# Threshold attention and hash routing: the identity ahead of tau, and routing's operations at other places

## The chip, the cores and the metric

The kernel runs on one core of one Trainium2 chip. Its metric is the device time of one execution, in microseconds (us). Lower is better. The kernel before takes 1007.04 us, the median of three runs that lie between 1006.65 and 1007.51. The profile comes from one more execution with a span of 1001.3 us.

The engines are named as in the profile: PE is TensorE (PEld its weight loads), DVE VectorE, ACT ScalarE, POOL GpSimd, SP SyncE, which issues most transfers. L219 is line 219 of the kernel before; in the changed kernel the same statement can stand some lines higher.

## The reference, cut to what matters

Attention in which all scores further than tau below the row's maximum are dropped, and then a layer of eight experts, in which each token goes to the one expert that a hash of its id names:

```python
scores = scale * np.matmul(q, k.transpose(0, 1, 3, 2))          # (8, 8, 576, 576), head_dim 64
thresh = np.max(scores, axis=-1, keepdims=True) - tau
scores = np.where(scores >= thresh, scores, -1000000000.0)
scores = scores - np.max(scores, axis=-1, keepdims=True)
attn = np.exp(scores)
attn = attn / (np.sum(attn, axis=-1, keepdims=True) + 1e-09)
x = np.matmul(attn, v)                                          # then to (4608, 512)
...
expert_idx = token_ids * np.int64(2654435761) % np.int64(E)     # E = 8
for e in range(E):
    mask = expert_idx == e
    h = np.maximum(x[mask] @ w1[e], 0.0)                        # 512 -> 1024
    out[mask] = h @ w2[e]                                       # 1024 -> 512
```

tau is 0.02 in the inputs. A negative tau drops everything; the kernel provides for that with a scale of 0 on k and a large value in `drop`.

## The kernel before: the parts concerned

The kernel treats heads in 32 pairs, each in five steps s = 0 to 4 (n counts all steps, p = n // 5). VectorE negates the scores and takes their extreme (`negate`), ScalarE takes the exponential (`expo`), VectorE masks (`mask`), TensorE turns the weights and multiplies them by v. The routing of the tokens to the experts is computed on the side, in pieces of a generator that hands back control at each `yield`; a second generator writes the token table when the slots are `placed`.

k is scaled by 1/8, or by 0 where tau is negative. Pair 0's k is scaled on VectorE and ScalarE at the start, all later ones on GpSimd:

```python
def scale_k(p):
    nc.gpsimd.tensor_scalar(out=kts[p][:], in0=kts[p][:], scalar1=keep_any[:],
                            scalar2=SCALE, op0=ALU.mult, op1=ALU.mult)
...
# in negate(n, j), after the tile of the last head: the threshold, on GpSimd too
    nc.gpsimd.tensor_scalar(out=thr[:, 0:j + 1], in0=stats[n][0][:, 0:j + 1],
                            scalar1=drop[:], scalar2=None, op0=ALU.add)
```

The start. `make_identity` is two operations on GpSimd. The transposes of the identity keep TensorE busy until there is something to do:

```python
load_pair(1)
make_identity(nc, ident[:])
...                                   # memsets on VectorE
with tc.manual_schedule():
    tr = ps_tr.tile([P, 2, 512], FP32, name="tr")
    for _ in range(16):
        nc.tensor.transpose(tr[:, 0, 0:P], ident[:], ident[:])
    nc.gpsimd.dma_start(out=tau_in[:], in_=...)
    nc.vector.tensor_scalar(out=keep_any[:], in0=tau_in[:], scalar1=0.0, scalar2=None,
                            op0=ALU.is_ge)
    nc.vector.tensor_scalar(out=drop[:], in0=keep_any[:], scalar1=-3e38, scalar2=3e38,
                            op0=ALU.mult, op1=ALU.add)
    nc.vector.tensor_tensor(out=drop[:], in0=drop[:], in1=tau_in[:], op=ALU.max)
    nc.vector.tensor_scalar(out=k_scale[:], in0=keep_any[:], scalar1=SCALE, scalar2=None,
                            op0=ALU.mult)
    nc.vector.tensor_scalar(out=kts[0][:, 0], in0=kts[0][:, 0], scalar1=k_scale[:], ...)
    nc.scalar.activation(kts[0][:, 1], kts[0][:, 1], AF.Copy, scale=k_scale[:])
    constants()
    next(pieces)
    score(0, 0)
```

The order on GpSimd in the built program is: first operation of the identity, tau's transfer, second operation of the identity.

Routing's last pieces make the table of overflow tiles `ov_i`, which is read at the very end of the kernel (and by SyncE's queue as soon as it is there):

```python
    placed.append(True)
    yield
    yield
    nc.vector.tensor_tensor(out=oc, in0=iota_f..., in1=oend..., op=ALU.is_ge)
    yield
    yield
    nc.vector.reduce_sum(ovf[:, 0:NOV], oc, axis=AX.X)
    yield
    nc.vector.tensor_scalar(out=ovf[:, 0:NOV], ..., op0=ALU.min)
    yield
    nc.vector.tensor_copy(ovf[:, NOV:NOV + 1], oend[:, E - 1:E])
    nc.vector.tensor_copy(ov_i[:], ovf[:])
```

In the loop a piece is taken twice in each pair, at s = 3 as the step begins and at s = 0 behind `negate` and `expo`, ahead of `put_xm` (L336). The passage to the experts follows the loop. There the first expert's first product (`early_h`, L579) is computed from the three quarters of x that are there, through the two PSUM buffers of `ps_sc`:

```python
for g in range(4):
    nc.vector.tensor_copy(gidx_x[rows, 1:, 0:n], stok[rows, 1:, KT * g:KT * g + n])
for kt in range(KT):
    fetch_0(kt, HP - 1)
fill(FO * 2 * (CO - 1) - 18)          # TensorE: early_h; VectorE takes each tile out (L586)
```

The memsets of `xh` and `o_last` (L765, L769) stand outside the fixed order and are placed among VectorE's work there.

Of the kernel before, what the change touches and what calls it, by code (L numbers as in the profile page):

```python
# [9 lines left out]
FP32 = mybir.dt.float32  # L10
# [4 lines left out]
ALU = mybir.AluOpType  # L15
# [5 lines left out]
def kernel(  # L21
# [12 lines left out]
    nc = tc.nc  # L34
# [51 lines left out]
    slot_i = consts.tile([P, NTC], I32, name="slot_i")  # L86
    tid32 = consts.tile([P, NTC, 2], I32, name="tid32")
    tau_in = consts.tile([P, 1], FP32, name="tau_in")
    keep_any = consts.tile([P, 1], FP32, name="keep_any")
    k_scale = consts.tile([P, 1], FP32, name="k_scale")  # L90
    drop = consts.tile([P, 1], FP32, name="drop")

# [35 lines left out]
    with tc.tile_pool(name="a_q", bufs=1) as a_q, \  # L128
# [67 lines left out]
                nc.sync.dma_start(out=v_sb[half, 4, half], in_=rows[TAIL:S, half])  # L196

        def scale_k(p):
            nc.gpsimd.tensor_scalar(out=kts[p][:], in0=kts[p][:], scalar1=keep_any[:],
                                    scalar2=SCALE, op0=ALU.mult, op1=ALU.mult)  # L200

        def heads(n):
            return 1 if n % NS == 0 else 2
# [314 lines left out]
                                      offset=0, ap=[[2 * NTC, P], [2, NTC], [1, 2]]))  # L518
        load_v(0)
        load_pair(1)  # L520
        make_identity(nc, ident[:])
        none_f = a_st.tile([P, 1], FP32, name="none_f")
        nc.vector.memset(none_f[:], 0.0)
        for w in w_bufs:
# [9 lines left out]
        def constants():  # L534

            nc.gpsimd.iota(iota_i[:], pattern=[[1, NOV]], base=0, channel_multiplier=0)
            nc.gpsimd.tensor_copy(iota_f[:], iota_i[:])
            make_upper_triangular(nc, u128[:], val=1.0, diag=False)
            nc.gpsimd.memset(ones128[:], 1.0)
            nc.gpsimd.memset(none[:], BIG)  # L540
            nc.gpsimd.memset(gidx[:], BIG)
            nc.gpsimd.memset(gidx_x[:], BIG)
            for t in sidx:
                nc.gpsimd.memset(t[:], BIG)
            nc.gpsimd.iota(tok[:], pattern=[[1, NTC]], base=0, channel_multiplier=NTC)
            for table in slot_dram:
                nc.sync.dma_start(out=table.rearrange("(p c) o -> p (c o)", p=P), in_=none[:])
# [69 lines left out]
                next(h_pieces, None)  # L617

        with tc.manual_schedule():

            tr = ps_tr.tile([P, 2, 512], FP32, name="tr")
            for _ in range(16):
                nc.tensor.transpose(tr[:, 0, 0:P], ident[:], ident[:])
            nc.gpsimd.dma_start(out=tau_in[:],
                                in_=bass.AP(tensor=tau.tensor, offset=0, ap=[[0, P], [1, 1]]))

            nc.vector.tensor_scalar(out=keep_any[:], in0=tau_in[:], scalar1=0.0, scalar2=None,
                                    op0=ALU.is_ge)  # L630
            nc.vector.tensor_scalar(out=drop[:], in0=keep_any[:], scalar1=-3e38, scalar2=3e38,
                                    op0=ALU.mult, op1=ALU.add)
            nc.vector.tensor_tensor(out=drop[:], in0=drop[:], in1=tau_in[:], op=ALU.max)
            nc.vector.tensor_scalar(out=k_scale[:], in0=keep_any[:], scalar1=SCALE, scalar2=None,
                                    op0=ALU.mult)
            nc.vector.tensor_scalar(out=kts[0][:, 0], in0=kts[0][:, 0], scalar1=k_scale[:],
                                    scalar2=None, op0=ALU.mult)
            nc.scalar.activation(kts[0][:, 1], kts[0][:, 1], AF.Copy, scale=k_scale[:])
            constants()
            next(pieces)  # L640
            score(0, 0)
            for n in range(LAST + NS + 1):
                p, s = divmod(n, NS)
                m = n - 2
                if s == 0 and p + 2 < NP:
                    load_pair(p + 2)
                if s == 0 and p + 1 < NP:
                    load_v(p + 1)
                if s == 2 and p in (20, 24):
                    load_w1(p // 4 - 5)  # L650
                if s == 2 and p in (22, 26):
                    load_w2((p - 22) // 4)

                if s == 3 and n < LAST:
                    next(pieces, None)
                if s == 1 and 3 <= p < 2 + KT:
                    nc.sync.dma_start(out=xg_bufs[p - 2][:], in_=xg_bufs[0][:])

                if s == 1 and 2 + KT <= p < 2 + KT + N // DIN:
                    r0 = DIN * (p - 2 - KT)  # L660
                    nc.sync.dma_start(
                        out=x_dram[r0:r0 + DIN, DIN - P:].rearrange("(t p) m -> p t m", p=P),
                        in_=xg_bufs[0][:].rearrange("p (t m) -> p t m", m=P))
                q = p - 1
                if s == 1 and 0 <= q < NP:
                    add_eps(q)
                if s == 1 and p + 1 < NP:
                    scale_k(p + 1)
                if s == 2 and 0 <= q < NP:
                    nc.vector.reciprocal(recs[q][:], recs[q][:])  # L670
                if n == LAST + NS:
                    fill(2)
                if s == 0 and p >= 2:
                    turn_o()
                if n == LAST:
                    for k in (0, 2):
                        tr = ps_sc.tile([P, 2, 512], FP32, name="sc")
                        early_xT(tr, k, k + 2, 0, CO - 1)
                if s in (1, 2) and 0 <= q < NP and n != LAST + 1:
                    av_part(q, 0, ((0, 1, 2), (3, 4))[s - 1])  # L680
                if n < LAST and s in (1, 2):
                    negate(n, 0)
                    expo(n, 0)
                if s == 2 and 0 <= q < NP:
                    put_oT(0)
                if n > LAST:
                    fill(1)
                turned = 0 <= m < LAST
                if turned:
                    tr = turn_w(m, 0)  # L690
                    put_wT(m, 0, tr)
                if n == LAST:
                    put_xm(p - 2)
                    av_part(q, 0, (0, 1, 2))
                if n >= LAST:
                    fill(1)
                if n == LAST:
                    tr = ps_sc.tile([P, 2, 512], FP32, name="sc")
                    early_xT(tr, 4, 5, 0, CO - 1)
                if s in (3, 4) and 0 <= q < NP:  # L700
                    av_part(q, 1, ((0, 1, 2), (3, 4))[s - 3])
                if n < LAST and s not in (1, 2):
                    negate(n, 0)
                    expo(n, 0)
                if s == 0 and n < LAST:
                    next(pieces, None)
                if s == 0 and p >= 2 and n != LAST:
                    put_xm(p - 2)
                if s == 4 and 0 <= q < NP:
                    put_oT(1)  # L710
                if s in (3, 4) and turned:
                    tr = turn_w(m, 1)
                if n + 1 < LAST:
                    score(n + 1, 0)
                if s == 4 and turned:
                    put_wT(m, 1, tr)
                if n < LAST and heads(n) == 2:
                    negate(n, 1)
                    expo(n, 1)
                if s == 3 and turned:  # L720
                    put_wT(m, 1, tr)
                if n + 1 < LAST:
                    score(n + 1, 1)
                if s in (0, 1) and turned:
                    tr = turn_w(m, 1)
                    put_wT(m, 1, tr)
                if 0 < n <= LAST:
                    for j in range(heads(n - 1)):
                        mask(n - 1, j)
                if s != 1 and placed:  # L730
                    next(scatter_pieces, None)


                if n >= G0 and s > 1 and early:
                    assert routed
                    fetch_0(*early.pop(0))
                if n == LAST:
                    fill(1)
            assert not early
            nc.vector.tensor_tensor(out=stok[:], in0=stok[:], in1=stok_odd[:], op=ALU.min)  # L740
            for h in range(4):
                rows, n = slice(32 * h, 32 * h + 32), (NB - h + 3) // 4
                nc.vector.tensor_copy(gidx[rows, :, 0:n], stok[rows, :, h::4])
            for g in range(4):
                rows, n = slice(32 * g, 32 * g + 32), min(KT, NB - KT * g)
                nc.vector.tensor_copy(gidx_x[rows, 1:, 0:n], stok[rows, 1:, KT * g:KT * g + n])
            for kt in range(KT):
                fetch_0(kt, HP - 1)
            fill(FO * 2 * (CO - 1) - 18)
            tr = ps_tr.tile([P, 2, 512], FP32, name="tr")  # L750
            early_xT(tr, 0, KT, CO - 1, CO)
# [195 lines left out]
```

## Time and profile before

| | of the profiled execution |
|---|---|
| span | 1001.3 us |
| TensorE busy | 983.8 us (98%) |
| VectorE busy | 517.7 us (52%) |
| ScalarE busy | 436.9 us (44%) |
| GpSimd busy | 291.7 us (29%) |
| scaling of k on GpSimd (L199) | 31 times, median 747 ns |
| routing's tail on VectorE: L468, L473, L475, L478, L479 | 412, 407, 274, 142, 183 ns |
| first and last of these in the span | 211.38 and 239.69 us |

A share of busy time is an average over the stages[...]. What a part of the change can bring is read where that part stands: at the start, in the steps of the attention stage, and at the passage to the experts.

### The profile page before, as it was taken

What the parts mean: (1) busy time and instruction counts of PE and PEld (TensorE: products, weight loads), DVE (VectorE), ACT (ScalarE), POOL (GpSimd) and SP (SyncE); (2) the same over time, 40 slices, a digit from 0 to 9 for tenths busy, and PEclk for the clock granted to TensorE, in tenths of its full rate; (3) what the DMA queues carried; (4) which work ended last, traced back from release to release, by engine and by line L of the source; (5) the groups of instructions that cost most, each with busy time, mean ns of one, the idle gap of its engine ahead of it and who ended that gap; (6) DMA issues with size and microseconds to landing.
All of it is one profiled execution on the core that took longest, in us unless ns stands there. A gap on an engine that the chain in (4) does not pass through costs nothing.

```text
span 1001.3 us, 20487 instructions
## 1 busy us (share of the span) xinstructions
PE 983.8 (98%) x7562; PEld 653.9 (65%) x7562; DVE 517.7 (52%) x1378; ACT 436.9 (44%) x714; POOL 291.7 (29%) x413
## 2 busy tenths in 40 slices
PE   7999999999999999999999999999999999999995
PEld 4666666666666666666766857768578577685773
DVE  7999999999999999994311010010101100200000
ACT  5988888888988889883200000010010000100000
POOL 3233323377676335550321030030210300300101
PEclk9999999999999999999999999999999999999998
DMA  7355544564467677410166344272352533801001
GB/s 182 74 129 141 129 117 112 136 141 107 92 185 169 154 195 194 114 49 25 39 189 185 116 105 143 91 211 89 106 163 84 158 91 104 222 1 39 27 10 57
DMA packets 145779, 117.07 MB, mean 117 GB/s; under 512 B 59860, under 2 KB 120280, under 8 KB 145680
## 3 DMA queue, kind: packets, MB, share of 16 engines
q1 hardware_dynamic: 135408, 96.41, 37.9%
q0 software_dynamic: 7824, 18.91, 6.1%
q8 instruction: 61, 1.00, 0.4%
q10 hardware_dynamic: 2448, 0.44, 0.2%
q14 instruction: 38, 0.31, 0.1%
HBM read 81.99 MB, written 22.37 MB: 104 GB/s over the span
## 4 chain that ended last, share of the span: by engine, by line
PE 87%; issue 6%; SPq 2%; DMA 2%; ACT 1%; DVE 1%; POOL 0%; POOLq 0%; ACTq 0%
PE sc L784 20%; PE av L297 17%; PE sc L219 15%; PE o_ps L802 12%; PE tr L266 10%; PE sc L815 8%; PE sc L579 3%; SPq L835 2%; PE av L266 1%; DMA out_dram<-o_last,gidx 1%; DMA out_dram<-o,gidx 1%; ACT w L244 1%; PE xT_ps L596 0%; PE sc L596 0%; ACT wT_a L287 0%
## 5 line engine op out<-in xcount | busy, mean ns | idle before, releaser
L244 ACT ACTIVATE w<-ns,nmx 128x576 f32<-128x576 f32 x288 | 220.3, 776 | 33.2 <-DVE ns L230 33.1
L784 PE MATMUL sc<-xT,w_sb 128*128 128x304 f32 x896 | 230.4, 419 | 0.0
L255 DVE SCALAR_TENSOR_TENSOR w<-ns,thr,w 128x576 f32<-128x576 f32 x288 | 225.4, 814 | 0.4 <-POOL thr L237 0.4
L784 PEld LDWEIGHTS sc<-xT,w_sb 128*128 128x128 f32 x896 | 170.2, 190 | 61.4 <-issue 3.3
L230 DVE TENSOR_SCALAR_CACHE_REDUCE ns<-sc 128x576 f32<-128x576 f32 x288 | 205.2, 744 | 6.3 <-PE sc L219 5.6
L219 PE MATMUL sc<-k_sb,q 64*128 64x288 f32 (+1 forms) x1280 | 179.2, 426 | 0.6 <-DVE ns L230 0.4
L802 PE MATMUL o_ps<-w_sb,h 128*128 128x512 f32 (+2 forms) x400 | 166.2, 575 | 0.0
L266 PEld LDWEIGHTS tr<-ident,w 64*128 64x128 f32 x2624 | 106.6, 139 | 88.7 <-ACT wT_b L287 26.3
L237 POOL TENSOR_SCALAR thr<-nmx,drop 128x2 f32<-128x2 f32 (+1 forms) x160 | 101.8, 637 | 176.7 <-DVE ns L230 163.4
L792 DVE TENSOR_SCALAR h<-sc 128x608 f32<-128x608 f32 x28 | 22.2, 791 | 240.9 <-PE sc L784 240.9
L266 PE MATMUL tr<-ident,w 64*128 64x64 f32 x2624 | 139.3, 231 | 2.7 <-ACT wT_a L287 2.0
L804 ACT COPY o<-o_ps 128x512 f32<-128x512 f32 (+2 forms) x25 | 14.2, 569 | 274.5 <-PE o_ps L802 248.1
L802 PEld LDWEIGHTS o_ps<-w_sb,h 128*128 128x128 f32 x400 | 74.9, 190 | 86.8 <-issue 84.7
L841 POOL DMA_INDIRECT out_dram<-o,gidx x24 | 23.9, 996 | 324.0 <-ACT o L804 291.4
L219 PEld LDWEIGHTS sc<-k_sb,q 64*128 64x128 f32 (+1 forms) x1280 | 93.0, 179 | 22.9 <-DVE ns L230 9.7
L297 PE MATMUL av<-wT_a,v 128*64 128x320 f32 (+1 forms) x704 | 100.4, 418 | 0.0
L790 ACT ACTIVATE h<-sc 128x608 f32<-128x608 f32 x28 | 19.0, 677 | 182.0 <-PE sc L784 182.0
L815 PE MATMUL sc<-h,w_sb 128*128 128x224 f32 x512 | 98.2, 352 | 0.0
L815 PEld LDWEIGHTS sc<-h,w_sb 128*128 128x128 f32 x512 | 96.9, 190 | 1.1
L287 ACT COPY wT_a<-tr 128x512 f32<-128x512 f32 (+1 forms) x128 | 81.7, 638 | 20.7 <-PE tr L266 20.1
L287 ACT COPY wT_b<-tr 128x512 f32<-128x512 f32 (+1 forms) x128 | 81.2, 634 | 6.4 <-PE tr L266 4.0
L297 PE MATMUL av<-wT_b,v 128*64 128x256 f32 x640 | 83.2, 389 | 0.0
(118 smaller groups left out, 547.9 us busy)
## 6 DMA issues: line engine op xcount, KB each, us to landing
w_sb<-in_moe_w_dram SPq DMA_DIRECT2D x16, 2048.0 KB
q<-in_q_dram SPq DMA_DIRECT2D x62, 288.0 KB
v<-in_v_dram SPq DMA_DIRECT2D x32, 256.0 KB
x_scratch<-xm SPq DMA_DIRECT2D x32, 256.0 KB
xT<-xq SPq DMA_DIRECT2D x84, 80.0 KB
k_sb<-in_k_dram SPq DMA_DIRECT2D x31, 144.0 KB
k_sb<-in_k_dram SPq DMA_DIRECT2D x32, 112.0 KB
o_last<-oq SPq DMA_DIRECT2D x210, 16.0 KB
```

The source lines that it names most:

```text
L219: nc.tensor.matmul(sc[out_rows, i, 0:S2], lhsT=q_sb[rows, h, q0:q1], rhs=k_sb[rows, h], start=True, stop=True)
L230: nc.vector.tensor_scalar(out=ns[:].rearrange("p (i s) -> p i s", i=2), in0=sc[:, :, 0:S2], scalar1=-1.0, scalar2=None, op0=ALU.mult, op1= ...
L237: nc.gpsimd.tensor_scalar(out=thr[:, 0:j + 1], in0=stats[n][0][:, 0:j + 1], scalar1=drop[:], scalar2=None, op0=ALU.add)
L244: nc.scalar.activation(w, nss[n, j][:], AF.Exp, bias=stats[n][0][:, j:j + 1], scale=-1.0)
L255: nc.vector.scalar_tensor_tensor(out=w, in0=nss.pop((n, j))[:], scalar=stats[n][1][:, j:j + 1], in1=w, op0=ALU.is_le, op1=ALU.mult, accum_ ...
L266: nc.tensor.transpose(dst[:, r, 64 * c:64 * c + 64], src[rows, c0:c0 + P], ident[rows, rows])
L287: nc.scalar.copy(dst, tr[:, :, 0:64 * n_c].rearrange("p r (c q) -> p r c q", c=n_c))
L297: nc.tensor.matmul(av[64 * j:64 * j + 64, g, c0:c1], lhsT=v_sb[:, c, 64 * j:64 * j + 64], rhs=wT[g][:, i, c0:c1], start=(c == 0), stop=stop)
L579: nc.tensor.matmul(h_ps[:, i, 0:CH], lhsT=w1_sb[:, co, fo * P:fo * P + P], rhs=xT_0[:, co, i * CH:i * CH + CH], start=(co == 0), stop=(co ...
L784: nc.tensor.matmul(h_ps[:, i, 0:width], lhsT=w1_sb[:, co, fo * P:fo * P + P], rhs=xT[:, co, i * width:i * width + width], start=(co == 0), ...
L802: nc.tensor.matmul(o_ps[:, 0:width], lhsT=h_sb[:, fo, FIRST[kt]:FIRST[kt] + P], rhs=w2_sb[:, fo, cols], start=(fo == 0), stop=(fo == FO - 1))
L815: nc.tensor.matmul(oT_ps[:, i, c * OW:c * OW + OW], lhsT=w2_sb[:, fo, co * P:co * P + P], rhs=h_sb[:, fo, FIRST[KF]:CAP], start=(fo == ord ...
```

## The change

The identity's two operations now both stand ahead of tau's transfer on GpSimd, so TensorE can begin to turn it earlier, and it turns it 17 times instead of 16. `k_scale` is computed from tau in one operation of VectorE instead of two (three stood there in the order of issue), and `drop` is computed after pair 0's k has been scaled, in a form that doesn't need `keep_any`. GpSimd scales the later pairs by `k_scale` and by 1.0, so the operation keeps its two operations. Routing's pieces begin in pair 1 at s = 3 instead of in pair 0, and they end when the slots are placed; the pieces after that, the overflow table, are taken in the passage, behind the copies of `gidx_x`. Nothing else is computed differently.

```diff
         def scale_k(p):
-            nc.gpsimd.tensor_scalar(out=kts[p][:], in0=kts[p][:], scalar1=keep_any[:],
-                                    scalar2=SCALE, op0=ALU.mult, op1=ALU.mult)
+            nc.gpsimd.tensor_scalar(out=kts[p][:], in0=kts[p][:], scalar1=k_scale[:],
+                                    scalar2=1.0, op0=ALU.mult, op1=ALU.mult)
...
         load_pair(1)
-        make_identity(nc, ident[:])
...
         with tc.manual_schedule():
+            make_identity(nc, ident[:])
 
             tr = ps_tr.tile([P, 2, 512], FP32, name="tr")
-            for _ in range(16):
+            for _ in range(17):
                 nc.tensor.transpose(tr[:, 0, 0:P], ident[:], ident[:])
             nc.gpsimd.dma_start(out=tau_in[:],
                                 in_=bass.AP(tensor=tau.tensor, offset=0, ap=[[0, P], [1, 1]]))
 
-            nc.vector.tensor_scalar(out=keep_any[:], in0=tau_in[:], scalar1=0.0, scalar2=None,
-                                    op0=ALU.is_ge)
-            nc.vector.tensor_scalar(out=drop[:], in0=keep_any[:], scalar1=-3e38, scalar2=3e38,
-                                    op0=ALU.mult, op1=ALU.add)
-            nc.vector.tensor_tensor(out=drop[:], in0=drop[:], in1=tau_in[:], op=ALU.max)
-            nc.vector.tensor_scalar(out=k_scale[:], in0=keep_any[:], scalar1=SCALE, scalar2=None,
-                                    op0=ALU.mult)
+            nc.vector.tensor_scalar(out=k_scale[:], in0=tau_in[:], scalar1=0.0, scalar2=SCALE,
+                                    op0=ALU.is_ge, op1=ALU.mult)
             nc.vector.tensor_scalar(out=kts[0][:, 0], in0=kts[0][:, 0], scalar1=k_scale[:],
                                     scalar2=None, op0=ALU.mult)
             nc.scalar.activation(kts[0][:, 1], kts[0][:, 1], AF.Copy, scale=k_scale[:])
+            nc.vector.tensor_scalar(out=drop[:], in0=tau_in[:], scalar1=0.0, scalar2=3e38,
+                                    op0=ALU.is_lt, op1=ALU.mult)
+            nc.vector.tensor_tensor(out=drop[:], in0=drop[:], in1=tau_in[:], op=ALU.max)
...
-                if s == 3 and n < LAST:
-                    next(pieces, None)
+                if s == 3 and p > 0 and not placed:
+                    next(pieces)
...
-                if s == 0 and n < LAST:
-                    next(pieces, None)
+                if s == 0 and p > 1 and not placed:
+                    next(pieces)
...
                 nc.vector.tensor_copy(gidx_x[rows, 1:, 0:n], stok[rows, 1:, KT * g:KT * g + n])
+            for _ in pieces:
+                pass
             for kt in range(KT):
                 fetch_0(kt, HP - 1)
```

In the built program VectorE's order in the passage is, behind the last copy of `gidx_x`: the compare (L468), a memset of `xh`, the sum (L473), the other memset of `xh`, the minimum (L475), the copy (L478), the memset of `o_last`, the cast of `ov_i` (L479), and then the evictions L586. Before it was: two memsets of `xh`, an eviction L586, the memset of `o_last`, the other evictions.

## The prediction

> **What bounds the kernel now.** I read the page first: the busy slices and the chain that ended last. The attention stage fills the first 45% of the span, the expert stage the rest.
>
> ```profile
> PE   7999999999999999999999999999999999999995
> DVE  7999999999999999994311010010101100200000
> ...
> PE 87%; issue 6%; SPq 2%; DMA 2%; ACT 1%; DVE 1%; POOL 0%; POOLq 0%; ACTq 0%
> ```
>
> TensorE is full in all but the first and last slice, and 87% of the chain runs on it. VectorE is as full, but only until slice 18. So outside the first slice a change counts where it lets TensorE wait less, and VectorE work in the attention stage counts only as far as it makes TensorE wait. The change touches three places, and I looked at each in the order of time.
>
> The first is the start, in the timeline (start us, length us, engine, line, operation):
>
> ```profile
> 1.48 0.74 POOL L624 DMA_DIRECT2D tau_in<-in_tau_dram  x1 [0.38 <-issue]
> 2.32 0.32 POOL masks.py:199 TENSOR_SCALAR_AFFINE_SELECT ident<-ident 128x128 f32<-128x128 f32 x1
> 2.69 3.67 PE L623 MATMUL tr<-ident 128*128 128x128 f32 x16 [2.69 <-POOL ident masks.py:199]
> 4.65 0.15 DVE L629 TENSOR_SCALAR keep_any<-tau_in 128x1 f32<-128x1 f32 x1 [1.41 <-DMA tau_in<-in_tau_dram]
> 5.28 0.54 ACT L638 ACTIVATE k_sb<-k_sb,k_scale 128x288 f32<-128x288 f32 x1 [0.48 <-DVE k_scale L634]
> 6.30 2.89 PE L219 MATMUL sc<-k_sb,q 64*64 64x288 f32 x16
> ...
> 11.64 0.75 POOL L199 TENSOR_SCALAR k_sb<-k_sb,keep_any 128x576 f32<-128x576 f32 x1 [2.86 <-DMA k_sb<-in_k_dram]
> 12.71 0.82 DVE L255 SCALAR_TENSOR_TENSOR w<-ns,thr,w 128x576 f32<-128x576 f32 x1 [0.40 <-POOL thr L237]
> 14.20 0.18 DVE L380 TENSOR_SCALAR eid<-tid 128x36 int32<-128x36 int32 x1
> 14.40 0.18 DVE L382 CAST eidf<-eid 128x36 f32<-128x36 int32 x1
> ```
>
> The first score starts at 6.30, when the 16 warming transposes are through; pair 0's k was scaled by 5.82 (5.28 + 0.54). The start of the kernel is then caught up by something else. At 12.71 the mask waits for its threshold, which stands behind the scaling of pair 1's k on GpSimd, and that waited 2.86 us for a transfer. The chain, in order of time, goes back from there through SyncE's queue of issues to 0.84 us; tau and the identity are not in it. From 12.71 on it runs through VectorE with the two routing operations at 14.20 and 14.40 in it, then over ScalarE to TensorE at 18.52, and stays on TensorE.
>
> The second is the granted clock, by stretches of 2 us (busy us by engine, then the clock, DMA share, GB/s):
>
> ```profile
> 16.00:18.00 2.00, 1.21 (x14) 0.62 (x12) 2.00 (x5) 1.44 (x4) 0.79 (x1) 1.00 1.05 255
> 18.00:20.00 2.00, 1.48 (x18) 0.80 (x18) 2.00 (x7) 1.90 (x4) 0.72 (x1) 0.68 1.21 235
> 20.00:22.00 2.00, 2.00 (x18) 1.41 (x16) 1.81 (x7) 1.57 (x3) 0.63 (x1) 0.50 1.00 241
> 22.00:24.00 2.00, 2.00 (x24) 1.28 (x22) 2.00 (x7) 1.30 (x3) 1.17 (x4) 0.97 1.10 221
> ```
>
> TensorE, 60% busy in the first row, loses half its clock for a while just when it becomes the bound.
>
> The third is the passage from attention to the experts:
>
> ```profile
> 470.96 16.64 PE L579 MATMUL sc<-xT,w_sb 128*128 128x304 f32 x64
> 474.46 1.03 DVE L765 MEMSET xh<- 128x512 f32 x2 [0.17 <-issue]
> 475.40 0.73 DVE L586 COPY h<-sc 128x608 f32<-128x608 f32 x1
> 476.29 0.91 DVE L769 MEMSET o_last<- 128x1024 f32 x1 [0.16 <-issue]
> 477.41 0.79 DVE L586 COPY h<-sc 128x608 f32<-128x608 f32 x1 [0.20 <-PE sc L579]
> ```
>
> TensorE runs the early first product without a gap. Its result leaves PSUM through two buffers, each emptied by VectorE (L586).
>
> [...] the lost share in the rows above, (0.32 + 0.50 + 0.03) × 2 us, at half rate is 3.4 us of throttle. [...] the trace has the threshold start at 12.39 as the k scaling ahead of it ends. [...] tau's 0.5 KB took 3.1 us here[...].
>
> **The change, part by part.**
>
> Start. tau's issue (0.74 us on GpSimd) goes behind the identity's second operation. The identity was ready at 2.64; its first operation ends at 1.10, so I let the second start between 1.2 and 1.5 and end by 1.5 to 1.8. The transposes begin about 1 us earlier; 17 at 3.67/16 = 0.229 us are 3.9 us, so they end at about 5.5 to 5.8. tau is issued about 0.4 us later and lands at about 5.0 instead of 4.58. Ahead of k's scaling then stands one operation of 0.15 us, where three of them stood between 4.65 and 5.28; the scaling starts at about 5.2 and ScalarE ends it at about 5.75. The first score starts at about 5.85, 0.45 us earlier. But pair 1's k lands at 11.45 as before, so the mask at 12.71 stays: VectorE, which now waits 0.40 there, would wait about 0.85. Worth to the end: 0.
>
> Routing's first operations leave pair 0. From 14.20 the next operation started at 14.50; in the changed kernel it starts at 14.20. This is on the chain: **−0.3 us**. The onehot of pair 1 (28.54, 0.45 us) moves too, but TensorE's step there was 13.85 us, no longer than a plain one, so that is worth nothing.
>
> Routing's tail leaves the attention stage. To price it I took the start of the first attention-times-v group of each pair in TensorE's timeline. In plain pairs (275.15 to 344.65, five of them) the step is 13.90 us, while VectorE has about 0.25 us of slack in it: nine score tiles at 0.68 + 0.74 us from start to start, 0.74 for xm and 0.13 for the reciprocal make 13.65. The five tail operations (412, 407, 274, 142 and 183 ns by the groups) stand between 211 and 240 us; the four steps from 205.25 to 261.25 are 13.93, 14.03, 14.20 and 13.84, together 0.40 above plain ones. I take **−0.35 us**. The routing that stays runs three half-pairs later with the same operations; the thirteen steps before those lie together about 1.7 us above plain ones and should do so again, give or take 0.4, since light and heavy halves are swapped.
>
> The tail goes to the passage. In the changed kernel's order of VectorE, after the copies of gidx_x, stand: compare, memset, sum, memset, minimum, copy, the big memset of o_last, the cast of ov_i, and only then the eviction of the early product's third tile; before, two memsets stood there, and o_last came after that eviction. From the last index copy's end at 474.28: 0.34 + 0.47 + 0.34 + 0.47 + 0.20 + 0.14 + 0.85 + 0.12 (durations of the rows less some 0.07 where the next starts early) is 2.9 us, so that eviction starts at about 477.2 instead of 475.40 and ends at about 478.0. TensorE needs this buffer for its fifth tile at about 477.2: the row at 470.96 holds 32 steps of two matmuls, 0.52 us each, six to a tile, so the third tile is done at 474.1 and the fourth at 477.2, which the wait at 477.41 confirms. So TensorE waits about 0.85 us, and all after it is TensorE's chain: **+0.85 us**. The last gathers are issued at 481 and landed about 3.8 us later, before TensorE asks for them at 487.5, so they don't hide it.
>
> The k scaling on GpSimd keeps shape and two operations: 31 of 747 ns, 0. SyncE's load of ov_i (0.47 us) moves from 240 to the passage, where that queue idles 31 us before L861: 0.
>
> Sum: −0.3 − 0.35 + 0.85 = +0.2 us, before the clock.
>
> **The clock.** TensorE starts earlier and then idles longer ahead of 13.7[...]. [...] VectorE waited 0.79 us for TensorE at 25.70, so about 0.8 us is the most that can come back quickly[...]. I give it one chance in three: −0.3 us on average. That makes 1006.9.
>
> **Rivals.**
> 1. The start counts in full: −0.45 more, and 1006.4. For it: the first score is the first real work. Against it: the waits at 11.64 and 12.71 name a transfer that the change doesn't touch.
> 2. The passage costs nothing, because the scheduler's order is not what VectorE is short of there: 1006.0. For it: VectorE has long idle stretches on both sides (7.20 us ahead of 464.69). Against it: the order is fixed and two buffers give only one tile of 3.1 us to recover.
> 3. The clock's dip vanishes and the passage costs: 1007.04 + 0.2 − 1.2 = 1006.0; together with the second rival, 1005.2.
> 4. Routing's new halves collide with xm (0.82 us, also in the first half of a pair), or the late scatters and slot reads push a transfer: up to +1, 1008. Against it: scatters ran from 200 to 323 with plain steps of 13.90 in their second half, and loads run two pairs ahead.
>
> **Range and chances.** All terms are below 1 us; three runs of the kernel before spread by 0.86 us. The range 1005.3 to 1008.2 covers the rivals. 2% would be 20 us, which nothing here can reach: faster 0.01, same 0.98, slower 0.01.
>
> **What would show it.** In the changed kernel's profile: transposes start before 2 us and the first score near 5.85; the mask still waits for its threshold near 12.7, longer than 0.40; no L380 at 14.2; steps of 13.90 right after routing ends; in the passage a wait of TensorE's early product for L586 of 0.6 to 1.0 us. I am wrong if TensorE shows no wait there, if the first mask comes earlier by the 0.45, or if routing's steps grow by over 0.5 in sum.

## The result

The changed kernel takes 1015.46 us, the median of six runs, and the kernel before 1007.47 us beside it. The ratio is 1.0074, with an interval of 1.0061 to 1.0087. The change is 7 to 8 us slower, where the prediction had 0.1 us faster and at most 1.2 us slower.

The page of the changed kernel (busy slices, and the chain that ended last) looks like that of before:

```profile
PE   7999999999999999999999999999999999999995
DVE  7999999999999998995431010110110100100000
...
PE 86%; issue 6%; DMA 2%; SPq 2%; ACT 1%; DVE 1%; POOL 0%; POOLq 0%; DVEq 0%; ACTq 0%
```

TensorE is still what everything waits for, and VectorE still fills the attention stage; slices of 25 us don't show 8 us. The statements stand one to three lines higher here: L219 is L218, L230 is L229, L255 is L254, L336 is L335.

The start, in the timeline of the changed kernel:

```profile
1.53 3.89 PE L622 MATMUL tr<-ident 128*128 128x128 f32 x17 [1.53 <-POOL ident masks.py:199]
...
5.77 1.57 PE L218 MATMUL sc<-k_sb,q 64*64 64x288 f32 x12 [0.35 <-DVE drop L633]
...
12.80 0.82 DVE L254 SCALAR_TENSOR_TENSOR w<-ns,thr,w 128x576 f32<-128x576 f32 x1 [1.61 <-POOL thr L236]
...
13.77 0.47 PE L265 MATMUL tr<-ident,w 64*128 64x64 f32 x8 [1.77 <-DVE w L254]
...
14.28 0.75 DVE L229 TENSOR_SCALAR_CACHE_REDUCE ns<-sc 128x576 f32<-128x576 f32 x1
```

The transposes start at 1.53, the first score at 5.77, and the mask stands at 12.80 all the same: the wait for the threshold took up the half microsecond. The operation behind it starts at 14.28 instead of 14.50, because the two routing operations are gone.

The passage to the experts:

```profile
488.82 0.12 DVE L478 CAST ov_i<-ovf 128x33 int32<-128x33 f32 x1
488.85 1.47 DVE L584 COPY h<-sc 128x608 f32<-128x608 f32 x2
489.68 10.50 PE L577 MATMUL sc<-xT,w_sb 128*128 128x304 f32 x40 [0.67 <-DVE h L584]
```

The early product, one run of 16.64 us before, is now cut in two: TensorE waits for the eviction that stands behind `ov_i`. From the beginning of the long run to the transposes behind it (L553) it is 17.51 us (482.60 to 500.11), where it was 16.57 (470.96 to 487.53).

These are the places the prediction had looked at, and they behave as it said. The time went elsewhere. To find it I marked each pair by the start of ScalarE's copy of `oT` (128x320, s = 2). The first mark is pair 1's. Interval 1 runs from pair 1's copy at s = 2 to pair 2's, so it holds pair 1 at s = 3 and pair 2 at s = 0. A plain interval is 13.90 us. The two profiles shown so far are no good pair for such sums, as the fourth group of runs shows, so here is the comparison from two runs on one chip:

| us, on one chip | kernel before (c_before) | changed (c_after) | difference |
|---|---|---|---|
| first mark | 28.25 | 27.97 | −0.28 |
| intervals 1 to 12: routing | 168.62 | 171.51 | +2.89 |
| intervals 13 to 22: slot table scattered | 141.59 | 142.70 | +1.11 |
| intervals 23 to 25 | 41.75 | 41.98 | +0.23 |
| intervals 26 to 31: early gathers | 87.70 | 89.85 | +2.15 |
| early product to the transposes behind it | 16.57 | 17.50 | +0.93 |
| all else | | | −0.1 |
| span | 1005.5 | 1012.4 | +6.9 |

### The profile page after: what moved, and what is told of

The parts are those of the page before. It is cut to its first block, busy times and chain, and to the rows that moved or that the text cites. A ratio compares the mean times of both kernels' runs of the same rounds, so it can differ in the third digit from the quotient of the medians.

```text
span 1013.9 us, 20494 instructions
## 1 busy us (share of the span) xinstructions
PE 992.3 (98%) x7563; PEld 657.1 (65%) x7563; DVE 520.4 (51%) x1377; ACT 438.6 (43%) x714; POOL 290.8 (29%) x413
## 4 chain that ended last, share of the span: by engine, by line
PE 86%; issue 6%; DMA 2%; SPq 2%; ACT 1%; DVE 1%; POOL 0%; POOLq 0%; DVEq 0%; ACTq 0%
PE sc L783 19%; PE av L296 17%; PE sc L218 14%; PE o_ps L801 12%; PE tr L265 10%; PE sc L814 8%; PE sc L577 2%; SPq L834 2%; PE av L265 1%; DMA k_sb<-in_k_dram 1%; DMA out_dram<-o_last,gidx 1%; DMA out_dram<-o,gidx 1%; ACT w L243 1%; PE xT_ps L594 0%; PE sc L594 0%
## 5 line engine op out<-in xcount | busy, mean ns | idle before, releaser
L254 DVE SCALAR_TENSOR_TENSOR w<-ns,thr,w 128x576 f32<-128x576 f32 x288 | 225.6, 816 | 4.9 <-POOL thr L236 4.9
L229 DVE TENSOR_SCALAR_CACHE_REDUCE ns<-sc 128x576 f32<-128x576 f32 x288 | 205.7, 747 | 10.1 <-PE sc L218 8.5
L218 PE MATMUL sc<-k_sb,q 64*128 64x288 f32 (+1 forms) x1280 | 182.4, 428 | 1.5 <-DVE ns L229 1.1
L803 ACT COPY o<-o_ps 128x512 f32<-128x512 f32 (+2 forms) x25 | 14.2, 569 | 274.5 <-PE o_ps L801 223.0
L218 PEld LDWEIGHTS sc<-k_sb,q 64*128 64x128 f32 (+1 forms) x1280 | 94.0, 179 | 25.1 <-DVE ns L229 10.4
```

What stands on the lines that cost most here:

```text
L218: nc.tensor.matmul(sc[out_rows, i, 0:S2], lhsT=q_sb[rows, h, q0:q1], rhs=k_sb[rows, h], start=True, stop=True)
L229: nc.vector.tensor_scalar(out=ns[:].rearrange("p (i s) -> p i s", i=2), in0=sc[:, :, 0:S2], scalar1=-1.0, scalar2=None, op0=ALU.mult, op1= ...
L254: nc.vector.scalar_tensor_tensor(out=w, in0=nss.pop((n, j))[:], scalar=stats[n][1][:, j:j + 1], in1=w, op0=ALU.is_le, op1=ALU.mult, accum_ ...
```

## The experiments

Each run is timed beside the kernel before on the same chip. The runs of one group shared a chip. The first four groups had different ones; the fifth is recorded with the chip number of the fourth.

### Which part carries it

Four kernels, each with a part of the change. e_start is the changed kernel with routing put back to where it was. e_routing is the kernel before with

```diff
-                if s == 3 and n < LAST:
-                    next(pieces, None)
+                if s == 3 and p > 0 and not placed:
+                    next(pieces)
...
-                if s == 0 and n < LAST:
-                    next(pieces, None)
+                if s == 0 and p > 1 and not placed:
+                    next(pieces)
...
+            for _ in pieces:          # in the passage
+                pass
```

e_later has only the conditions on p, so all pieces stay in the loop; e_tail has only `not placed` and the two lines in the passage.

> The changed kernel's start alone: identity ahead of tau, 17 transposes, one operation ahead of k's scaling; routing as in the kernel before. Theory A (the start makes TensorE idle longer ahead of 13.8 us, [...] and the engines settle in a slower rhythm): most of the 8 us are here, +6 to +8 us, steps of 14.1 to 14.3 us from the first pairs on[...]. Theory B (routing, which now runs three half-pairs later, shifts the rhythm): within 1 us of the kernel before, steps of 13.90.

> The kernel before with routing as in the changed kernel: its pieces begin in pair 1 and the overflow table is made in the passage; the start is the old one. Theory A: the passage's +0.9 us and little else, +0.3 to +1.5 us. Theory B: +6 to +8 us, with steps of 14.1 to 14.3 us and the long wait of GpSimd's first gather for the store of xm.

> The kernel before with routing's pieces begun three half-pairs later, all of them in the loop, so that the slots are placed and scattered later, but nothing is added to the passage. Theory A: -0.3 to +0.5 us. Theory B: +5 to +7 us, as the passage has nothing to do with it. Theory C (late placing alone makes the gathers and the stores of xm collide near 405 us): +3 to +5 us, with steps of 13.90 until then.

> The kernel before with the overflow table alone moved to the passage; routing begins in pair 0 as before. All theories: +0.5 us (0.85 to 0.95 us of waiting in the passage less up to 0.4 us of the five operations in the attention stage), with TensorE's early product waiting 0.6 to 1.0 us for VectorE's eviction there. If the time doesn't move, the passage costs nothing by itself.

| | ratio to before, interval | intervals 1–12 | 13–22 | 26–31 |
|---|---|---|---|---|
| e_start | 1.0007 (0.9998 to 1.0015) | 168.61 | 142.17 | 88.70 |
| e_tail | 1.0002 (0.9994 to 1.0011) | 168.58 | 141.84 | 88.26 |
| e_later | 1.0060 (1.0047 to 1.0073) | 171.44 | 142.91 | 90.84 |
| e_routing | 1.0058 (1.0045 to 1.0071) | 171.46 | 142.89 | 90.69 |

One of the 14 timed executions of e_start took 3932 us, for a reason that the record does not show; it is left out of the ratio.

My first suspicion, theory A, was the start: the trace of the changed kernel has TensorE's clock halved (0.50 granted) for 6.83 us from 15.96, where the first one of before has 3.41 us. It falls. The start alone changes nothing that can be measured, though its trace too has 6.83 us of half clock. Routing's place carries nearly all (theory B), and the passage is no part of that, since e_later, without it, is as slow as e_routing. C falls as the only cause, because the excess begins at interval 1.

### Later, or in the other half of the pair?

The shift by three half-pairs does two things: everything comes later, and the pieces change places. The long ones (onehot, the scans, the additions) stood at s = 3 and now stand at s = 0 ahead of xm. e_half is later by one half-pair, which swaps the places; e_pair is later by a whole one, which doesn't. e_s4 takes at s = 4 the piece that was taken at s = 0. That was meant to move the short pieces alone, but it does something else, as shown below. e_g0 is the changed kernel with its early gathers a pair later.

```diff
 e_half   -                if s == 0 and n < LAST:
          +                if s == 0 and p > 0 and n < LAST:
 e_pair   -                if s == 3 and n < LAST:
          +                if s == 3 and p > 0 and n < LAST:
          -                if s == 0 and n < LAST:
          +                if s == 0 and p > 0 and n < LAST:
 e_s4     -                if s == 0 and n < LAST:
          +                if s == 4 and n < LAST:
 e_g0     -        G0 = NS * ((HP - 1) * B + 2)
          +        G0 = NS * ((HP - 1) * B + 3)
```

> The kernel before with routing's pieces one half-pair later, nothing else: the long pieces (onehot, the scans, the additions over 288 values), which stood at s = 3, now stand at s = 0 ahead of xm, and the short ones at s = 3. Theory P (a piece at s = 0 costs its whole length, one at s = 3 next to nothing): twelve steps of pairs 1 to 12 are together 2.5 to 3.2 us longer than in the kernel before, and the time is +2 to +3.5 us. Theory L (it is the later slot table that costs, through scatters and gathers): +0 to +1 us, and pairs 1 to 12 as before.

> The kernel before with routing's pieces a whole pair later, so that each piece stands in the same half as before and only the slot table comes one pair later. Theory P: pairs 1 to 12 take as long in sum as before (+-0.5 us), the time +0 to +1 us. Theory L: +3 to +5 us, most of it at pairs 25 to 28.

> The changed kernel with its early gathers begun one pair later (the start of the gathers moves from step 0 of pair 26 to step 0 of pair 27, fifteen gathers as before), so that the first doesn't wait for its indices. If the collision of late indices, gathers and stores of xm at pairs 26 and 27 is a cause of its own: 3 to 4.5 us faster than the changed kernel, so +3 to +5 us against the kernel before, and no step over 14.6 us at pairs 26 and 27. If it only moves with the gathers: as the changed kernel, +7 us, with a step over 15 us one pair later.

> The kernel before with the short pieces moved from s = 0 to s = 4 (behind negate and expo of the first tile), the long ones staying at s = 3. Theory P: the short ones cost up to 0.35 us each at s = 0, 1.5 us together, and little at s = 4, so the time is -0.5 to -1.5 us and the steps of pairs 1 to 12 lie together below 168.0 us (168.6 before). If s = 4 is as tight as s = 0: no change, -0.3 to +0.5 us.

| | ratio to before, interval | intervals 1–12 | 26–31 |
|---|---|---|---|
| e_pair | 1.0009 (1.0000 to 1.0018) | 168.26 | 89.25 |
| e_half | 1.0037 (1.0024 to 1.0050) | 171.69 | 89.55 |
| e_s4 | 1.0030 (1.0018 to 1.0041) | 170.37 | 87.81 |
| e_g0 | 1.0043 (1.0028 to 1.0057) | 171.50 | 88.38 |

Half a pair costs more than a whole pair. Every kernel with its long pieces at s = 3 and its short ones at s = 0 has 168.3 to 168.6 us in intervals 1 to 12, and every one with them the other way round has 171.4 to 171.7. One can follow it piece by piece:

| piece | interval with it at s = 3 (c_before) | with it at s = 0 (c_after) |
|---|---|---|
| onehot | 13.95 | 14.27 |
| first scan | 13.91 | 14.25 |
| second scan | 13.98 (row copy at s = 0 beside it) | 14.26 |

The timelines show why. First c_before, from pair 1 at s = 3 to pair 2 at s = 1 (L385 is onehot; the lines are VectorE's but for one):

```profile
29.04 0.45 DVE L385 TENSOR_TENSOR onehot<-eidf,iota_f 128x288 f32<-128x288 f32 x1
29.41 0.75 DVE L230 TENSOR_SCALAR_CACHE_REDUCE ns<-sc 128x576 f32<-128x576 f32 x1
...
32.42 0.76 DVE L230 TENSOR_SCALAR_CACHE_REDUCE ns<-sc 128x576 f32<-128x576 f32 x1
...
35.32 0.76 DVE L230 TENSOR_SCALAR_CACHE_REDUCE ns<-sc 128x576 f32<-128x576 f32 x1
36.01 0.82 DVE L336 TENSOR_TENSOR xm<-av,rec 128x640 f32<-128x640 f32 x1
...
39.29 1.19 PE L219 MATMUL sc<-k_sb,q 64*128 64x288 f32 x8
```

And the kernel with routing half a pair later (c_half, on the same chip):

```profile
29.19 0.76 DVE L230 TENSOR_SCALAR_CACHE_REDUCE ns<-sc 128x576 f32<-128x576 f32 x1
...
32.40 0.76 DVE L230 TENSOR_SCALAR_CACHE_REDUCE ns<-sc 128x576 f32<-128x576 f32 x1 [0.29 <-PE sc L219]
...
35.30 0.76 DVE L230 TENSOR_SCALAR_CACHE_REDUCE ns<-sc 128x576 f32<-128x576 f32 x1
35.98 0.45 DVE L385 TENSOR_TENSOR onehot<-eidf,iota_f 128x288 f32<-128x288 f32 x1
36.35 0.82 DVE L336 TENSOR_TENSOR xm<-av,rec 128x640 f32<-128x640 f32 x1
...
39.38 1.44 PE L219 MATMUL sc<-k_sb,q 64*128 64x288 f32 x8
```

VectorE's longest wait here is ahead of the first tile of s = 4 (32.40, 0.29 us), for TensorE's scores. In c_before onehot at s = 3 takes up part of that wait, and s = 4 begins at the same time (32.42). Behind it VectorE runs through s = 0 to 2 with a gap of only 0.05 us, at the first tile of s = 0. At s = 0 onehot moves xm by 0.37 us, every operation after it by as much, and the group of scores at 39.38, which needs a buffer that `negate` empties, takes 1.44 us instead of 1.19 and starts 0.09 later. TensorE has then lost 0.34 us (40.82 against 40.48), and as it is what bounds the kernel, it doesn't get them back: interval 1 is 14.33 us in c_half and 13.95 in c_before.

The first profile of the kernel before has the wait in a pair without routing, too:

```profile
270.22 0.08 DVE L255 DVE_READ_ACCUMULATOR w<-ns,thr,w 128x1 f32 x1
270.36 0.76 DVE L230 TENSOR_SCALAR_CACHE_REDUCE ns<-sc 128x576 f32<-128x576 f32 x1
...
273.20 0.08 DVE L255 DVE_READ_ACCUMULATOR w<-ns,thr,w 128x1 f32 x1
273.25 0.76 DVE L230 TENSOR_SCALAR_CACHE_REDUCE ns<-sc 128x576 f32<-128x576 f32 x1
```

Elsewhere in the pair a tile starts together with the accumulator read that closes the mask before it (both at 276.15, both at 281.28). Here it starts 0.14 us later at s = 4 and 0.05 us later at s = 0.

One interval has another cause. The copy of the counts, a short piece, stands at s = 3 in the changed kernel, and waits there for TensorE's two small products (c_after):

```profile
100.51 0.17 DVE L409 COPY cnt<-av 128x16 f32<-128x16 f32 x1 [0.50 <-PE av L407]
```

Its interval takes 14.77 us; with the copy at s = 0, in c_before, it takes 14.25. So about 0.5 us of the 2.89 come from this wait.

e_s4 was a miss: I expected a gain, and it is 3 us slower. But it doesn't do what its expectation says. The piece that it drops at s = 0 of pair 0 ran ahead of the first s = 3, so every piece comes one place later: the short ones stand at s = 3, and it is the long ones that stand at s = 4, behind the wait:

```profile
31.24 0.76 DVE L230 TENSOR_SCALAR_CACHE_REDUCE ns<-sc 128x576 f32<-128x576 f32 x1 [0.29 <-PE sc L219]
...
31.92 0.45 DVE L385 TENSOR_TENSOR onehot<-eidf,iota_f 128x288 f32<-128x288 f32 x1
```

The wait of 0.29 us is still there, and the interval takes 14.28 us, against 13.95 with onehot at s = 3. So e_s4 shows that a long piece just behind the wait is paid as well; what the short pieces alone would gain at s = 4 was not tested. e_g0 came out as expected in time, but not in its shape: interval 27 is still 15.35 us where I had at most 14.6.

### The same operation at both places, measured by itself

If that is right, an operation that has nothing to do with routing must behave the same. e_dum0 and e_dum3 add one in each of the last 15 pairs of the kernel before, at s = 0 ahead of xm, or at s = 3 as the step begins:

```diff
+                if s == 0 and p >= 17 and n < LAST:      # e_dum3: if s == 3 and p >= 17, at the step's beginning
+                    nc.vector.tensor_tensor(out=pad[:], in0=pad[:], in1=pad[:], op=ALU.mult)
```

e_fix is the changed kernel with one condition altered (`s == 0 and p > 0` instead of `p > 1`), which puts the long pieces at s = 3 again. e_two is a try at something better: new start, both pieces of a pair at s = 3 from pair 0 on, and the overflow table behind the early product.

> The kernel before with one more operation of VectorE (128x288 squared in place, about 0.37 us from start to start, read by nobody) in each of the last 15 pairs, at s = 0 ahead of xm. Theory P (VectorE has its only wait of a pair at s = 4, and from s = 0 until then TensorE runs right behind it): the whole length is paid, 13 to 15 x 0.3 to 0.37 us, +4 to +5.5 us. If a pair's slack of 0.25 us can be used anywhere: +1 to +2.5 us.

> The kernel before with the same additional operation in the same 15 pairs, at s = 3 as the step begins, ahead of VectorE's wait. Theory P: most of it goes into that wait, at most 0.1 us a pair is paid, 0 to +1.5 us. If a piece costs the same anywhere: as the run with it at s = 0.

> The changed kernel with routing's pieces half a pair earlier, so that each long piece stands at s = 3 again and the slot table comes one pair later than before, not one and a half. The early-product wait in the passage stays. Theory P with the late collision: pairs 1 to 12 at 168.3 to 168.8 us (171.5 in the changed kernel), pairs 26 to 31 at about 89 us (91.5), so 4 to 6 us faster than the changed kernel, +1 to +2.5 us against the kernel before. If halves don't matter: within 1.5 us of the changed kernel.

> A version meant to beat both: the changed kernel's start, routing from pair 0 with both pieces of a pair taken at s = 3 as the step begins (none at s = 0), and the overflow table behind the early product in the passage. Theory P: pairs 1 to 12 at 167.0 to 168.0 us, nothing in the passage, -0.5 to -2 us against the kernel before. If two pieces together overrun the wait of VectorE: 0 to +1 us.

| | ratio to before, interval | intervals 1–12 | 13–22 | 23–25 | 26–31 |
|---|---|---|---|---|---|
| e_dum0 | 1.0046 (1.0032 to 1.0059) | 168.54 | 141.92 | 42.80 | 88.26 |
| e_dum3 | 1.0005 (0.9997 to 1.0014) | 168.56 | 140.40 | 41.96 | 86.03 |
| e_fix | 1.0013 (1.0004 to 1.0021) | 168.30 | 139.16 | 41.73 | 87.69 |
| e_two | 1.0001 (0.9993 to 1.0009) | 168.82 | 139.04 | 41.74 | 86.74 |

Intervals 23 to 25 have no routing, no gathers and at most one scatter, and take 41.73 us in e_fix as in the first profile of the kernel before. One operation of 0.37 us in each costs 1.07 us at s = 0, 0.36 each, and 0.23 us at s = 3, 0.08 each. In the time it is 4.6 us against 0.5 us, by the ratios. The trace of e_dum0 shows why nothing is recovered: VectorE still waits at s = 4, though the pair has more work, and the operation stands behind that wait:

```profile
385.06 0.76 DVE L231 TENSOR_SCALAR_CACHE_REDUCE ns<-sc 128x576 f32<-128x576 f32 x1 [0.18 <-PE sc L220]
...
388.64 0.46 DVE L708 TENSOR_TENSOR pad<-pad 128x288 f32<-128x288 f32 x1
```

e_fix is the strongest: half a pair earlier, and the changed kernel comes to +0.13% from +0.74% (on another chip).

e_two gains nothing. The two small products of routing and the copy of their result came together at pair 5, where VectorE waited 0.49 us for TensorE, and that interval took 14.62 us.

### One chip for the sum, and the collision at the end

On the chip of e_fix the kernel before took 1003.8 us, on the others some 1008. The profile that I predicted from (span 1001.3) has 139.39 us in intervals 13 to 22 where e_tail and e_start have 142. To know what belongs to the chip I ran both kernels again, unchanged, with e_g0 and e_half repeated beside them.

> The kernel before, unchanged, with a profile of its own beside the next three on one chip. If the 14.2 us steps of pairs 13 to 22 belong to the chip: where its time is about 1008 us, they are here too (142 us for these ten steps), where it is about 1004 us, they are 13.9 us. If they belong to the change: 139.4 us in any case.

> The changed kernel, unchanged, on the same chip: +6 to +8.5 us, of which pairs 1 to 12 +2.9 us, pairs 13 to 22 within 1 us of the kernel before, pairs 26 to 31 +2 to +4 us, the passage +0.9 us.

> The changed kernel with its early gathers begun one pair later, on the same chip. If the collision is worth what the traces say: 2.5 to 4 us faster than the changed kernel here, +3.5 to +5 us against the kernel before.

> The kernel before with routing half a pair later, on the same chip: +2.9 us in pairs 1 to 12, and +3 to +4 us in the time.

c_before took 1007.5 us and has 141.59 us in intervals 13 to 22. So the slow steps while the slot table is scattered are there without the change, and are absent in the first profile of the same kernel. c_after is at 1.0070 (1.0057 to 1.0083), c_g0 at 1.0045 (1.0032 to 1.0058), c_half at 1.0038 (1.0025 to 1.0051).

The late part is intervals 26 to 31: 87.70 us in c_before, 89.85 in c_after, 88.29 in c_g0. In time, moving the gathers by a pair is worth 1014.42 − 1011.41 = 3.0 us by the medians; the intervals of the two ratios just overlap. In the two profiles, whose spans differ by 2.6 us, intervals 26 to 31 show 1.56 us of it. Another 1.27 lies at the first mark (26.70 us in c_g0, 27.97 in c_after), long before the gathers, where the half clock lasted 3.41 us in one and 6.83 in the other. What happens in this late part is seen in the timeline of the changed kernel (SPq is SyncE's queue of issues, L109 the gather of rows of x, L341 the store of xm, L124 a load of expert weights, L195 of v):

```profile
368.57 3.82 SPq L496 DMA_DIRECT2D sidx<-slot_scratch  x8
...
374.39 2.92 SPq L500 DMA_DIRECT2D stok_odd<-slot_scratch  x4
377.43 0.65 SPq L173 DMA_DIRECT2D k_sb<-in_k_dram  x1
...
382.68 0.54 SPq L341 DMA_DIRECT2D x_scratch<-xm  x1
...
384.46 0.59 SPq L124 DMA_DIRECT2D w_sb<-in_moe_w_dram  x1
...
388.54 1.14 POOL L109 DMA_INDIRECT xg<-x_scratch,gidx  x1 [4.43 <-DVE ns L229]
...
392.29 4.32 SPq L195 DMA_DIRECT2D v<-in_v_dram  x2
401.28 0.37 SPq L341 DMA_DIRECT2D x_scratch<-xm  x1
...
404.94 1.11 POOL L109 DMA_INDIRECT xg<-x_scratch,gidx  x1 [6.01 <-DMA x_scratch<-xm]
406.43 0.82 DVE L254 SCALAR_TENSOR_TENSOR w<-ns,thr,w 128x576 f32<-128x576 f32 x1 [2.38 <-POOL thr L236]
...
407.40 0.46 PE L265 MATMUL tr<-ident,w 64*128 64x64 f32 x8 [1.50 <-DVE w L254]
```

In the kernel before the same transfers stand like this:

```profile
334.24 4.17 SPq L497 DMA_DIRECT2D sidx<-slot_scratch  x8
...
374.22 0.54 SPq L342 DMA_DIRECT2D x_scratch<-xm  x1
...
376.01 0.59 SPq L125 DMA_DIRECT2D w_sb<-in_moe_w_dram  x1
...
378.93 1.13 POOL L110 DMA_INDIRECT xg<-x_scratch,gidx  x1 [0.94 <-DMA x_scratch<-xm]
```

The slot table is read back over SyncE's queue, which it holds for 8.7 us (368.57 to 377.31), and the pair's loads of k, q and v and the store of xm queue behind it. Before, this happened at pair 23, with two pairs to recover. Now it is at pair 25, right ahead of the gathers that need the store: VectorE starts xm at 377.33, and its store is issued at 382.68, 5.35 us later; before, it was 2.95 us (371.27 to 374.22). The gather comes late in its pair, the next store of xm waits 4.2 us for the gathers, and at 404.94 GpSimd has waited 6.01 us for that store with the threshold queued behind the gather. VectorE waits 2.38 us for it, and TensorE 1.50 us for VectorE.

That the table is read back right ahead of the gathers is not all of it. In c_half it is read back a pair earlier, from 354.19 to 363.04 us, and still GpSimd is idle for 4.66 us ahead of the first gather (389.35) and 5.81 ahead of the fourth. SyncE's queue carries something else there: an expert's weights, 2048 KB, issued right behind the store at 384.46 (376.01 before). In the changed kernel the load of v behind them waits 3.3 us for them, in c_g0 3.7; neither profile of the kernel before has such a wait between 366 and 412 us. No run separates the weights from the slot reads, so the cause of this part is read from traces and not isolated.

How much of this is due to lateness alone I can't fix to better than a microsecond. Of c_half's 3.8 us by the ratio, 0.8 are left when the 3.05 of its intervals 1 to 12 are taken off, though its profile has 90.21 us in intervals 26 to 31; the profiled execution was the slowest of its six (1013.67 us, median 1011.28). Intervals 26 to 31 differ by 1.7 us between two profiles of the changed kernel (89.85 in c_after and 91.53 in the first). Nearly all of that is interval 27, with 16.01 and 17.62 us: in the first one TensorE's clock was halved from 408.49 to 411.90, inside that interval, and in c_after it was not.

### The passage, and a second try at something better

e_pass is the changed kernel with the overflow table moved behind the early product. e_best is e_two with the copy of the counts one pair behind the products that make them.

```diff
-            for _ in pieces:
-                pass
             for kt in range(KT):
                 fetch_0(kt, HP - 1)
             fill(FO * 2 * (CO - 1) - 18)
             tr = ps_tr.tile([P, 2, 512], FP32, name="tr")
             early_xT(tr, 0, KT, CO - 1, CO)
+            for _ in pieces:
+                pass
```

> The changed kernel with the overflow table's operations moved from ahead of the early product's third eviction to behind the early product, nothing else. If the 0.93 us that TensorE loses in the passage come from them: no wait of the early product for VectorE's eviction, the stretch from the early product's long run to the transposes behind it 16.6 us (17.5 in the changed kernel), the time about 0.9 us below the changed kernel, +5.5 to +7 us against the kernel before.

> A second try at a version better than both: as the one with both pieces of a pair at s = 3, but the copy of the counts out of PSUM one pair behind the two small products that make them, so that VectorE doesn't wait for TensorE there. The overflow table stands behind the early product. Pairs 1 to 12 at 167.8 to 168.3 us, -0.3 to -1.5 us against the kernel before.

In e_pass the early product runs 16.64 us without a wait, and the stretch is 16.58 us again: the passage is settled at 0.93 us. Its ratio is 1.0058 (1.0045 to 1.0071); against the changed kernel's 1.0070 to 1.0074 the intervals overlap, so the time alone would not have shown it. e_best is at 0.9996 (0.9988 to 1.0004), with 168.52 us in intervals 1 to 12. It missed the 167.8 to 168.3 that I expected, and isn't faster than the kernel before by anything that can be measured. As I read it, two pieces together overrun VectorE's wait, and what is saved at s = 0 is paid at s = 3; no run isolates that.

## Why the prediction was wrong

The range was missed by 7 us. By its steps:

- **Start, worth 0**: right, and e_start shows it (1.0007, with 1 in the interval). First score, transposes and the mask near 12.7 came as written; the mask's wait was 1.61 us, not 0.85. That tau lands later by as much as it is issued later was my estimate: issued 0.16 us later (1.64 instead of 1.48), it is taken up 0.35 us later (5.00 instead of 4.65). Ahead of k's scaling the trace of before has four small operations (4.65, 4.83, 5.02 and 5.10), not three; the sum doesn't depend on it.
- **Routing's first operations leave pair 0, −0.3**: −0.28 at the first mark, between c_before and c_after, whose half clocks begin at nearly the same time (15.82 and 15.75); that is one pair of profiles.
- **Tail, −0.35**: right. On the chip without slow scatter steps, intervals 13 to 15 are 42.03 us with the tail in the loop (e_dum0) and 41.71 without it (e_two), 0.32 us.
- **Passage, +0.85**: right; 0.93 measured, and e_pass removes it.
- **The clock, −0.3 on average**: no effect of the change can be seen. With the old start and with the new one the stretch of half clock at the start lasted 0, 3.41 or 6.83 us (new: e_fix, e_two and the changed kernel). It differs between profiles of one and the same kernel: the kernel before has 3.41 us in one profile and 6.83 us in another, e_g0 6.83 and its repeat c_g0 3.41, and e_pair, with the start of before, none. That the change could move or shorten it was my estimate, which no run shows; the 1.2 us that the third rival gave to a dip that vanishes was one too.
- **The step that failed** is this one: "The routing that stays runs three half-pairs later with the same operations; the thirteen steps before those lie together about 1.7 us above plain ones and should do so again, give or take 0.4, since light and heavy halves are swapped." I saw the swap and priced it as a wash. The twelve intervals from c_before to c_after went from 1.8 to 4.7 us above plain ones, so it costs 2.9 us: at s = 3 a long piece goes into VectorE's wait, at s = 0 it is paid in full by TensorE; and about 0.5 us is the copy of the counts, which waits for TensorE at s = 3. The 0.25 us of slack that I computed for the pair is not spread over it. Most of it is one wait at one place, and the trace of before has it: the first tile of s = 4 starts 0.14 us late at 270.36 and again at 284.25. The last of my signs of being wrong, routing's steps growing by over 0.5 us in sum, is the one that came.
- **Rival 4** named the right mechanism for the rest, "the late scatters or slot reads push a transfer", and sized it at most 1 us. It is about 2: 2.15 us in intervals 26 to 31 between c_before and c_after. I argued against it that scatters ran beside plain steps and that loads run two pairs ahead; what I didn't follow was SyncE's queue, where the slot reads stand ahead of the store that the first gather needs, and the weights right behind it. Which of the two costs how much stays open.
- Intervals 13 to 22 carry +1.11 us in one pair of profiles. The last routing pieces lie at pairs 13 to 15 now, and the last scatter is issued in pair 23, at 348.81 us in c_after, not in pair 22, at 325.16 in c_before (interval 22: 14.65 us instead of 13.90). That is read from the trace, and not isolated by a run. Why the scatter steps take 14.2 us in some profiles and 13.9 in others of the same kernel stays open.

## What to carry to other kernels

Slack is a place before it is an amount. Where two engines have nearly the same work in a loop, find the one wait of the nearly full engine, and put side work just ahead of it, as much as fits; the same operation behind it was paid in full here by the engine that bounds the loop (0.36 of 0.37 us in e_dum0), and moving "the same work" by half a period cost 0.37% of the time (e_half), by a whole one 0.09% (e_pair). When work moves later, follow also the queues that it issues into: what stood far ahead of a consumer may now stand right in front of it.

## What the runs showed that I had not expected

- The same kernel differs by 4 us between chips (1003.8 and 1007.5 to 1008.4 us). The fast chip has no profile of the kernel before itself, but those of e_two, e_fix and e_dum3 have 139.0 to 140.4 us in the ten steps with scatters, against 141.6 and more in every profile from the chips of the other groups. The first profile, with 139.39, has no chip on record. A trace from one chip and a median from another are not to be subtracted from each other.
- An operation of VectorE of 0.45 us by the record moves the next by 0.37 us (onehot in c_half: it starts at 35.98, xm at 36.35), and it is the 0.37 that TensorE pays (0.36 each in e_dum0).
- Reading the slot table back in 16 transfers (eight of 0.5 to 0.6 KB and eight of 19 KB) holds SyncE's queue for 8.7 us. While it ran, the DMA engines were busy for 0.30 (368 to 372 us) and 0.34 (372 to 376 us) of the time; it was the issuing queue that was occupied, not the engines.
